# A linear-attention and RWKV feed-forward kernel: other places in the planner's table for about 450 tasks of the first units

## The chip, the cores and the metric

The kernel runs on one core of a Trainium2 chip. A core has five engines that run their own instruction streams: TensorE (PE, matmuls; PEld are its weight loads), VectorE (DVE), ScalarE (ACT), GpSimd (POOL) and SyncE (SP), which here issues all DMA transfers; 16 DMA engines move the data. The metric is the device time of one execution in microseconds (us).

## The reference

For 4 sequences, 8 heads, 768 steps and head size 48, a recurrent attention with a decay per channel is computed, and its output goes through an RWKV channel mix (shift, two mixes, a squared-ReLU feed-forward and a gate).

```python
def _attn_ref(q, k, v, f_logit):
    f = 1.0 / (1.0 + np.exp(-f_logit))
    for t in range(S):
        state = f[:, :, t, :, None] * state + np.einsum('bhd,bhe->bhde', k[:, :, t], v[:, :, t])
        y[:, :, t] = np.einsum('bhd,bhde->bhe', q[:, :, t], state)
def _moe_ref(x, mu_k, mu_r, w_k, w_v, w_r):      # x: (4, 768, 384), w_k: (384, 1024), w_v: (1024, 384)
    xk = mu_k * x + (1.0 - mu_k) * x_prev        # x_prev: x one step earlier
    xr = mu_r * x + (1.0 - mu_r) * x_prev
    k = np.maximum(xk @ w_k, 0.0)
    v = k * k @ w_v
    r = 1.0 / (1.0 + np.exp(-(xr @ w_r)))
    return r * v
```

The weights arrive as 64-bit floats.

## The kernel before, in words

The 4 x 768 steps are cut into 24 chunks of 128 steps (i = 0 to 23; all 8 heads at once), and three chunks make a unit of 384 steps (u = 0 to 7). Each chunk is computed in the parallel form; the state goes from chunk to chunk. Every small job is a task with a name, one engine or a choice of two, an estimated duration, and a place. The names that the text uses:

- Loads on SyncE's queue: `wr0` to `wr3`, `wk0` to `wk7`, `wv0` to `wv5` (pieces of the weights), `f0.0` to `f0.2`, `f1`, `f2` (decay logits of a unit), `qk{i}`, `v{i}` (a chunk's operands), `cst` (the unit matrix `ident` and the mask), `sp{u}.{j}` (small copies that spread two heads' output from `stage` into `x`).
- Weights, on VectorE: three integer operations a piece, as `wkS2`, `wkT2`, `wkX2` (lines 623, 632, 635), turn a 64-bit piece into 32-bit floats; then ScalarE rounds it (`wkH2`, line 638) and GpSimd takes the rest (`wkL2`, line 642). The last product needs `wvL5`.
- Attention of chunk i: `b{i}` scan of the decay and `bl{i}` its last column, `ln{i}`, `rb{i}` its inverse, `q{i}`, `n{i}`, `kr{i}`, `k{i}` scaled operands, `TR{i}` transposes of k (TensorE, line 310), `kt{i}` their copy (lines 314, 315), `SP{i}` scores and state sums (lines 325 and 345, 64 matmul records), `m{i}` the mask (line 337), `zb{i}`, `za{i}`, `T{i}` the state, `YA{i}` and `YB{i}` the output (line 362), with the small copy `w{i}` (lines 381, 382) between them, and `y{i}`, the copy of the output to `x` and `stage` (lines 394, 396).
- Mix of unit u: `d`, `xm` (lines 474, 477, 482), `xh` (rounded, lines 490, 491), `xl` (the rest, line 497). Products on TensorE (line 505): `F{u}.0` to `.7` with wk (9 records each), `R{u}.0` to `.2` with wr (9), `W{u}.00` to `.21` with wv (12); between them `r`, `h`, `kk`, `l` (squares), `lg`, `sg` (gate) and `o`, `out`. W0.01 is unit 0's first row block, second half.
- Fills (line 700): matmuls of `ident` by itself with no use, put into TensorE's waits.

Nothing is decided at run time. A planner (class `Plan`) runs while the program is built: `schedule` takes from all tasks whose predecessors are planned the one with the least key, and the order so found is fixed on every engine.

```python
self.tasks[name] = (name, place + PLACE.get(name, 0.0), ways, tuple(after), tuple(takes), tuple(uses))
...
k = (round((start + 0.2 * stay) / 0.15), place, n)
```

The start in the key is the planner's own estimate, in steps of 0.15; the place (about the number of the unit, less for what should come early) decides between tasks of one step. Where a task can run on two engines, `pick` takes the one that would end first, with `DEAR` added to VectorE's and ScalarE's ends. The buffers of each tag (four PSUM buffers `pm`, four operand buffers `qk`, two `words` buffers) are given out in the planned order, and a task waits until the buffer that it takes is free. The fills go in ahead of a TensorE task whose planned start leaves a gap; they start by `t = max(free["P"], read, FILL[0])`, which does not look at when `ident` lands.

Of the kernel before, what the change touches and what calls it, by code (L numbers as in the profile page):

```python
# [51 lines left out]
AWAY = 1  # L52
SPLIT = True
HALVED = 1
PLACE = {"f1": -0.627, "f2": 0.21, "sf2": -1.016, "qk0": 0.854, "qk1": -0.278, "qk2": 0.127, "qk3": 0.31, "v0": -0.151, "v1": -0.224, "cst": 0.482, "mu": 0.138, "f3": -1.807}
CHECK = (2.0, 0.2)
DEAR = {"V": 2.498, "A": 2.512}


class Plan:  # L60
# [8 lines left out]
    def add(self, name, place, *ways, after=(), takes=(), uses=()):  # L69
        assert name not in self.tasks, name  # L70
        self.tasks[name] = (name, place + PLACE.get(name, 0.0), ways, tuple(after), tuple(takes), tuple(uses))
        for b in (*takes, *uses):
# [11 lines left out]
    def schedule(self, trace=None):  # L84
# [23 lines left out]
        while ready:  # L108
            best = None
            for n, names in ready.items():  # L110
# [6 lines left out]
                at = {w[0]: max([at] + [0.0 if way_of[m] == w[0] else end[m] for m in names]) for w in ways}  # L117
                pick = min(((max(at[w[0]], free[w[0]]) + w[1] + DEAR.get(w[0], 0.0), w) for w in ways), key=lambda x: x[0])[1]
                start = max(at[pick[0]], free[pick[0]])
# [825 lines left out]
```

## Time and profile before

| | |
|---|---|
| Time, median of 3 runs | 357.0 us (356.54 to 357.54) |
| Span of the profiled execution | 354.9 us |
| The rest of the median, around the span | 2.1 us |
| TensorE busy | 323.3 us (91% of the span) |
| VectorE busy | 254.9 us (72%) |
| ScalarE busy | 204.8 us (58%) |
| GpSimd busy | 194.2 us (55%) |
| Mean granted clock of TensorE | 0.988 |

The span is the time from the first to the last instruction of one execution that was profiled; its own time was not taken apart from it, and the median of the three runs stands beside it. Shares are means over the whole span, and the stretches differ: in the first 75 us the weights are turned and the first chunks computed, later the products follow each other.

### The profile page before, as it was taken

How to read it: one execution, taken by the hardware profiler on the slowest of the kernel's cores; microseconds unless marked ns; L12 is line 12 of the kernel's file. 1: busy time of each engine (PE TensorE's matmuls, PEld its weight loads, DVE VectorE, ACT ScalarE, POOL GpSimd, SP SyncE). 2: the span in 40 equal slices, each digit the busy share in tenths (PEclk: the TensorE clock that was granted, in tenths of full speed). 3: DMA queues.
4: the chain of work that ended last, by engine and by line, in shares of the span. 5: the costliest groups of instructions: out<-in, count | busy, mean ns of one | idle time of the engine just before them, and what ended most of it. 6: DMA issues, size and time to landing. Idle time of an engine off the chain costs nothing.

```text
span 354.9 us, 10867 instructions
## 1 busy us (share of the span) xinstructions
PE 323.3 (91%) x4482; PEld 307.0 (87%) x4482; DVE 254.9 (72%) x511; ACT 204.8 (58%) x415; POOL 194.2 (55%) x235
## 2 busy tenths in 40 slices
PE   0395788999999999999999999999999999999993
PEld 0384677888899999999999999999999999999993
DVE  7978799989899878958897598748872943723210
ACT  4686458757476927863575547573876146605520
POOL 2554469986689347724595268625680634634400
PEclk9999699999999999999999999999999999999998
DMA  8999172336521284368524562031401100010001
GB/s 279 403 375 369 54 230 61 118 96 207 204 98 59 55 298 130 105 228 254 170 81 129 187 218 85 2 121 61 152 0 40 48 27 11 8 46 22 3 24 52
DMA packets 20650, 45.32 MB, mean 128 GB/s; under 512 B 2928, under 2 KB 13040, under 8 KB 20592
## 3 DMA queue, kind: packets, MB, share of 16 engines
q1 hardware_dynamic: 20592, 44.55, 37.8%
q8 instruction: 37, 0.61, 0.7%
q14 instruction: 21, 0.17, 0.2%
HBM read 38.64 MB, written 4.72 MB: 122 GB/s over the span
## 4 chain that ended last, share of the span: by engine, by line
PE 70%; DVE 13%; DMA 5%; ACT 4%; issue 3%; POOL 2%; SPq 1%; DVEq 0%; POOLq 0%; ACTq 0%
PE pm L505 56%; PE py L362 6%; PE pss L325 3%; PE pm L310 2%; DMA f<-in_zt 2%; PE pss L345 2%; DVE pm L632 2%; DVE pm L623 2%; DMA qk<-in_qkt 1%; DVE xm L482 1%; DMA words<-in_wv 1%; DVE words L635 1%; DVE xm L477 1%; DVE ss L337 1%; DVE xh L491 1%
## 5 line engine op out<-in xcount | busy, mean ns | idle before, releaser
L505 PE MATMUL pm<-xh,wk 128*128 128x384 f32 x384 | 105.5, 344 | 1.7 <-POOL wk L642 1.1
L505 PE MATMUL pm<-wv,k2h 128*128 128x384 f32 x384 | 98.8, 338 | 0.0
L543 POOL TENSOR_TENSOR k2l<-kk,k2h 128x384 fp32r<-128x384 f32 x64 | 68.1, 1066 | 37.4 <-DVE kk L535 16.3
L497 POOL TENSOR_TENSOR xl<-xm,xh 128x384 fp32r<-128x384 f32 x48 | 52.7, 1101 | 59.7 <-DVE xh L491 49.5
L505 PEld LDWEIGHTS pm<-xh,wk 128*128 128x128 f32 x384 | 69.8, 188 | 5.0 <-POOL wk L642 2.1
L505 PEld LDWEIGHTS pm<-wv,k2h 128*128 128x128 f32 x384 | 68.7, 188 | 0.2
L505 PE MATMUL pm<-xl,wk 128*128 128x384 f32 x192 | 64.6, 336 | 0.0
L505 PE MATMUL pm<-wv,k2l 128*128 128x384 f32 x192 | 64.5, 336 | 0.0
L528 ACT ACTIVATE r<-pm 128x384 f32<-128x384 f32 x54 | 26.5, 491 | 29.8 <-PE pm L505 29.1
L505 PE MATMUL pm<-wr,xh 128*128 128x384 f32 x144 | 38.0, 345 | 0.9 <-DVE words L635 0.9
L595 DVE TENSOR_TENSOR o<-pm,lg 128x384 f32<-128x384 f32 x24 | 13.3, 554 | 34.1 <-PE pm L505 34.1
L505 PEld LDWEIGHTS pm<-wv,k2l 128*128 128x128 f32 x192 | 36.1, 188 | 0.0
L505 PEld LDWEIGHTS pm<-xl,wk 128*128 128x128 f32 x192 | 36.1, 188 | 0.0
L535 DVE SCALAR_TENSOR_TENSOR kk<-pm,r 128x384 f32<-128x384 f32 x39 | 21.6, 555 | 19.6 <-ACT r L528 18.9
L533 ACT ACTIVATE k2h<-r 128x384 fp32r<-128x384 f32 x64 | 33.6, 524 | 3.7 <-DVE r L529 1.4
L240 DVE TENSOR_TENSOR_SCAN pm<-f,low 128x512 f32<-128x512 f32 x24 | 32.1, 1339 | 0.0
L362 PEld LDWEIGHTS py<-qk,z 64*64 64x64 f32 x704 | 16.8, 139 | 15.3 <-issue 7.5
L362 PE MATMUL py<-qk,z 64*64 64x64 f32 x704 | 23.1, 234 | 7.2 <-ACT stage L394 2.8
L394 ACT ACTIVATE x<-py 64x128 f32<-64x128 f32 (+1 forms) x60 | 18.6, 310 | 15.5 <-PE py L362 14.6
L505 PEld LDWEIGHTS pm<-wr,xh 128*128 128x128 f32 x144 | 25.2, 188 | 1.8 <-DVE words L635 1.0
L482 DVE SCALAR_TENSOR_TENSOR xm<-pm,mu_sb,x 128x384 f32<-128x384 f32 x42 | 25.7, 613 | 0.7
L700 PE MATMUL py<-ident 128*128 128x64 f32 x72 | 11.4, 322 | 14.6 <-DVE pm L240 14.6
(101 smaller groups left out, 569.1 us busy)
## 6 DMA issues: line engine op xcount, KB each, us to landing
qk<-in_qkt SPq DMA_DIRECT2D x24, 512.0 KB, 4.5
words<-in_wv SPq DMA_DIRECT2D x12, 512.0 KB, 4.8
f<-in_zt SPq DMA_DIRECT2D x7, 768.0 KB, 5.9
v<-in_vt SPq DMA_DIRECT2D x24, 192.0 KB, 3.1
out<-o SPq DMA_DIRECT2D x24, 192.0 KB, 2.5
words<-in_wk SPq DMA_DIRECT2D x6, 512.0 KB, 5.1
words_k2h<-in_wk SPq DMA_DIRECT2D x4, 384.0 KB, 8.6
words_k2l<-in_wk SPq DMA_DIRECT2D x4, 384.0 KB, 9.5
```

The source lines that it names most:

```text
L240: pl.add(f"b{i}", ga, ("V", 1.25, 1, lambda: nc.vector.tensor_tensor_scan(b().rearrange(FL), f().rearrange(FL), self.low.rearrange(FL), 1. ...
L362: first[c, h] = nc.tensor.matmul(to, lhs, rhs, start=(c, h) not in first, stop=stop, skip_group_check=True)
L394: e.activation(o, i_, AF.Copy, scale=-1.0)
L482: pl.add(f"xm{u}.{n}{j}", pr, ("V", 0.62, 0, lambda xm=xm, n=n, j=j: nc.vector.scalar_tensor_tensor(xm(), pm("d", u, j)[:, :UT], self.mu_s ...
L497: e.tensor_tensor(lo(), xm(), hi().bitcast(F32), op=ALU.subtract)
L505: nc.tensor.matmul(ps, lhs(a, j), rhs(bb, j), start=ends[0] and i == 0, stop=ends[1] and i == len(pr) - 1)
L528: pl.add(f"r{u}.{f}", kf, ("A", 0.5, 0, lambda r=r, ps=ps: nc.scalar.activation(r(), ps(), AF.Relu)), ("V", 0.56, 0, lambda r=r, ps=ps: nc ...
L533: pl.add(f"h{u}.{f}", kf, ("A", 0.53, 0, lambda r=r, hi=hi: nc.scalar.activation(hi(), r(), AF.Square)), after=[f"r{u}.{f}"], **kw)
L535: pl.add(f"kk{u}.{f}", kf, ("V", 0.56, 0, lambda r=r, ps=ps, kk=kk: nc.vector.scalar_tensor_tensor(kk(), ps(), 0.0, r(), op0=ALU.max, op1= ...
L543: e.tensor_tensor(lo(), kk(), hi().bitcast(F32), op=ALU.subtract)
L595: pl.add(f"o{u}.{t}", kv, ("V", 0.56, 0, lambda t=t, ps=ps, o=o: nc.vector.tensor_tensor(o(), ps(), lg()[:, t], op=ALU.mult)), after=[f"W{ ...
L700: self.nc.tensor.matmul(self.py[:, 0, 256:320], self.ident, self.ident[:, :64], start=False, stop=True, skip_group_check=True)
```

## The change

Two constants of the planner change, and no task, instruction, buffer or wait rule. `PLACE` held an offset for 12 tasks; now it holds one for about 450, in the attention of chunks 0 to 11, the weights, unit 0 and most of unit 1. `DEAR` changes in its second digit.

```diff
-PLACE = {"f1": -0.627, "f2": 0.21, "sf2": -1.016, "qk0": 0.854, "qk1": -0.278, "qk2": 0.127, "qk3": 0.31, "v0": -0.151, "v1": -0.224, "cst": 0.482, "mu": 0.138, "f3": -1.807}
+PLACE = {
+    "cst": 0.45, "ex": 7.598, "c0": 0.906, "cm0": -1.376, "c2": -1.069, "v0": -3.667, "b0": 0.122, "bl0": -1.422, "rb0": 0.016,
...
+    "YB3": 0.435, "y3": -4.0, "qk4": 1.56, "v4": -0.449, "b4": -0.062, "bl4": -1.34, "ln4": -1.489, "rb4": 2.257, "kr4": 3.283,
...
 CHECK = (2.0, 0.2)
-DEAR = {"V": 2.498, "A": 2.512}
+DEAR = {"V": 2.455, "A": 2.357}
```

What it moves is seen in the orders. (Line numbers of the changed program are 53 higher, since the table is longer.)

On SyncE's queue, the loads of the first microseconds before the change, from the first decay logits (`f`) on; the four pieces of `wr` (`lg` and `x` are their places) stand ahead of these rows:

```order
L410 DMA f_61<-in_zt 128x512 x3
L228 DMA qk_65<-in_qkt 128x1024
L230 DMA v_101<-in_vt 128x384
L410 DMA f_62<-in_zt 128x1536
L230 DMA v_102<-in_vt 128x384
L228 DMA qk_66<-in_qkt 128x1024
L706 DMA ident<-in_cst 128x128
L708 DMA mask<-in_cst 64x64 x2
L228 DMA qk_64<-in_qkt 128x1024
L230 DMA v_103<-in_vt 128x384
L410 DMA f_63<-in_zt 128x1536
```

and the same place after it, where two pieces of `wr` and `v0` stand ahead:

```order
L682 DMA lg_119<-in_wr 128x576 x2
L463 DMA f_61<-in_zt 128x512 x2
L281 DMA qk_65<-in_qkt 128x1024
L463 DMA f_61<-in_zt 128x512
L463 DMA f_62<-in_zt 128x1536
L281 DMA qk_64<-in_qkt 128x1024
L281 DMA qk_66<-in_qkt 128x1024
L283 DMA v_102<-in_vt 128x384
L283 DMA v_103<-in_vt 128x384
L463 DMA f_63<-in_zt 128x1536
L759 DMA ident<-in_cst 128x128
L761 DMA mask<-in_cst 64x64 x2
```

`ident` and the mask moved from behind `qk2` to behind `f2`; `qk0` moved ahead of them.

On TensorE, the output of chunk 2 and the scores of chunk 3 before the change; `qk_66` is chunk 2's operand, `qk_67` chunk 3's, and the rows from `z_72` on are YB2:

```order
L325 MATMUL pss<-qk_67 64x64 x16
L345 MATMUL pss<-v_101,ktk_100 48x48 x16
L362 MATMUL py<-qk_66,z_72 64x64
L362 MATMUL py<-qk_66,z_73 64x64 x2
L362 MATMUL py<-qk_66,z_72 64x64 x2
L362 MATMUL py<-qk_66,z_73 64x64 x2
L362 MATMUL py<-qk_66,z_72 64x64
L362 MATMUL py<-ss_97,v_103 48x64 x16
L362 MATMUL py<-qk_67,z_75 64x64
```

and after it:

```order
L415 MATMUL py<-qk_66,z_72 64x64
L415 MATMUL py<-qk_66,z_73 64x64 x2
L415 MATMUL py<-qk_66,z_72 64x64 x2
L415 MATMUL py<-qk_66,z_73 64x64 x2
L415 MATMUL py<-qk_66,z_72 64x64
L415 MATMUL py<-ss_97,v_102 48x64 x16
L378 MATMUL pss<-qk_67 64x64 x16
L398 MATMUL pss<-v_101,ktk_100 48x48 x16
L415 MATMUL py<-qk_67,z_75 64x64
```

YB2 now stands ahead of SP3, and so does the copy y2 that follows it. Up to YA2 TensorE's order is unchanged.

On VectorE, the end of chunk 5's operand and the start of unit 0's mix before the change (`ktk_99` is kt4, `qk_65` k5, `words_120` wvT0; `xm` and `xh` are the mix, `ss` and `z` m4 and zb4):

```order
L315 COPY ktk_99<-pm_92 128x384
L262 SCALAR_TENSOR_TENSOR qk_65<-pm_94,qk_65 128x2x128
L266 SCALAR_TENSOR_TENSOR qk_65<-pm_94,qk_65 128x2x64 x2
L632 SCALAR_TENSOR_TENSOR pm_93<-words_120,pm_93 128x512
L477 SCALAR_TENSOR_TENSOR xm_109<-x_105,one_mu,pm_91 128x384
L491 CAST xh_122<-xm_109 128x384
L337 TENSOR_TENSOR ss_97<-pss,mask 128x512
L296 TENSOR_TENSOR z_73<-pss,z_72 128x4x48
L477 SCALAR_TENSOR_TENSOR xm_110<-x_105,one_mu,pm_91 128x384
L491 CAST xh_122<-xm_110 128x384
L477 SCALAR_TENSOR_TENSOR xm_111<-x_105,one_mu,pm_92 128x384
L491 CAST xh_122<-xm_111 128x384
```

and after it:

```order
L315 SCALAR_TENSOR_TENSOR qk_65<-pm_94,qk_65 128x2x128
L319 SCALAR_TENSOR_TENSOR qk_65<-pm_94,qk_65 128x2x64 x2
L685 SCALAR_TENSOR_TENSOR pm_92<-words_120,pm_92 128x512
L530 SCALAR_TENSOR_TENSOR xm_109<-x_105,one_mu,pm_93 128x384
L530 SCALAR_TENSOR_TENSOR xm_110<-x_105,one_mu,pm_94 128x384
L530 SCALAR_TENSOR_TENSOR xm_111<-x_105,one_mu,pm_91 128x384
L390 TENSOR_TENSOR ss_97<-pss,mask 128x512
L349 TENSOR_TENSOR z_73<-pss,z_72 128x4x48
L355 TENSOR_TENSOR sm<-pss,z_73 128x192
L530 SCALAR_TENSOR_TENSOR xm_112<-x_105,one_mu,pm_94 128x384
L544 CAST xh_122<-xm_112 128x384
```

kt4 and three of the xh copies left VectorE for ScalarE. In the same way y5 and the small copy bl6 go to ScalarE, and kk0.7 comes to VectorE. Between the xm rows and wkX7 VectorE's list of weight pieces is the same but for wv4, which stands where wv2 stood. Further on, YB6, SP7 and YA7 come later among the products of units 0 and 1, and some 30 tasks of all units have another engine. Of the nine fills seven are left: five stood among F0.1 to F0.7, now three.

## Rows read from the trace of the kernel before

**Rows 1.** The page: busy us and instructions by engine; the instruction queue: packets, MB, share.
```profile
PE 323.3 (91%) x4482; PEld 307.0 (87%) x4482; DVE 254.9 (72%) x511; ACT 204.8 (58%) x415; POOL 194.2 (55%) x235
...
q8 instruction: 37, 0.61, 0.7%
```

**Rows 2.** Windows: busy us (instructions) per engine, granted TensorE clock, DMA share, GB/s.
```profile
36.00:39.00 3.00, 3.00 (x125) 3.00 (x125) 2.07 (x5) 0.55 (x1) 2.15 (x3) 0.53 0.07 23
...
75.00:350.00 275.00, 273.53 (x3568) 262.42 (x3566) 189.13 (x380) 155.18 (x313) 147.80 (x173) 1.00 0.31 102
```

**Rows 3.** Timeline of TensorE: start us, us, engine line op out<-in xcount [idle before].
```profile
14.57 3.65 PE L700 MATMUL py<-ident 128*128 128x64 f32 x16 [14.57 <-DVE pm L240]
...
19.08 1.97 PE L310 MATMUL pm<-ident,qk 128*128 128x128 f32 x8 [0.86 <-DVE qk L266]
...
29.74 0.66 PE L310 MATMUL pm<-ident,qk 128*128 128x128 f32 x4
...
30.55 0.46 PE L362 MATMUL py<-qk,z 64*64 64x64 f32 x16 [0.15 <-ACT done L381]
...
33.45 0.29 PE L362 MATMUL py<-qk,z 64*64 64x64 f32 x3 [0.58 <-DVE z L296]
...
35.91 0.59 PE L362 MATMUL py<-qk,z 64*64 64x64 f32 x11 [2.16 <-issue]
...
80.57 0.59 PE L505 MATMUL pm<-wv,k2h 128*128 128x384 f32 x2
...
95.39 0.45 PE L505 MATMUL pm<-xh,wk 128*128 128x384 f32 x1
```

**Rows 4.** Timeline of GpSimd.
```profile
79.37 1.31 POOL L642 TENSOR_TENSOR wv<-words,wv 128x512 fp32r<-128x512 f32 x1 [1.22 <-ACT wv L638]
...
93.40 1.78 POOL L497 TENSOR_TENSOR xl<-xm,xh 128x384 fp32r<-128x384 f32 x1 [0.36 <-DVE xh L491]
```

**Rows 5.** Timeline of VectorE.
```profile
38.16 0.69 DVE L337 TENSOR_TENSOR ss<-pss,mask 128x512 f32<-128x512 f32 x1 [0.22 <-PE pss L345]
...
43.31 0.56 DVE L315 COPY ktk<-pm 128x384 f32<-128x384 f32 x1 [0.48 <-PE pm L310]
...
45.10 0.61 DVE L477 SCALAR_TENSOR_TENSOR xm<-x,one_mu,pm 128x384 f32<-128x384 f32 x1
...
53.14 0.55 DVE L623 TENSOR_SCALAR pm<-words_k2l 128x384 int32<-128x384 int32 x1
...
74.31 1.04 DVE L396 TENSOR_SCALAR x<-py 128x256 f32<-128x256 f32 x3
...
76.40 0.69 DVE L623 TENSOR_SCALAR pm<-words 128x512 int32<-128x512 int32 x1 [0.74 <-DMA words<-in_wv]
...
77.92 0.69 DVE L635 SCALAR_TENSOR_TENSOR words<-words,pm 128x512 int32<-128x512 int32 x1
```

**Rows 6.** Timeline of SyncE's queue, two DMA issues.
```profile
7.29 0.33 SPq L706 DMA_DIRECT2D ident<-in_cst  x1
...
12.31 0.33 SPq L410 DMA_DIRECT2D f<-in_zt  x1
```

**Rows 7.** DMA issues from 7.2 and from 12.3 us: KB each, us to landing.
```profile
ident<-in_cst SPq DMA_DIRECT2D x1, 64.0 KB, 7.1
...
f<-in_zt SPq DMA_DIRECT2D x1, 768.0 KB, 5.9
```

**Rows 8.** The instruction queue in 33.4 to 33.5 and in 37.0 to 37.1 us.
```profile
q8 instruction: 1, 0.02, 68.0%
...
q8 instruction: 1, 0.02, 65.5%
```

**Rows 9.** Timeline of ScalarE: the copy y2 begins.
```profile
39.27 0.97 ACT L394 ACTIVATE x<-py 128x256 f32<-128x256 f32 x3 [1.34 <-PE py L362]
```

**Rows 10.** Tile xh on VectorE: ns min/median/max, first and last start.
```profile
L491 DVE CAST xh<-xm x36: 355/396/999, 45.7 to 312.3; 128x384 fp32r<-128x384 f32 x36
```

**Rows 11.** The chain that ended last: start us, us, what.
```profile
103.61 9.71 PE pm L505 x54
```

More of the change, by code (lines that the diff above doesn't have):

```diff
@@ L54 @@
 HALVED = 1
-PLACE = {"f1": -0.627, "f2": 0.21, "sf2": -1.016, "qk0": 0.854, "qk1": -0.278, "qk2": 0.127, "qk3": 0.31, "v0": -0.151, "v1": -0.224, "cst": 0.482, "mu": 0.138, "f3": -1.807}
+PLACE = {
[52 rows of a table added]
+}
 CHECK = (2.0, 0.2)
-DEAR = {"V": 2.498, "A": 2.512}
+DEAR = {"V": 2.455, "A": 2.357}
 class Plan:
```

50 rows, old and new, of the table PLACE are left out of this document.

## The prediction

> **What bounds the kernel now.** I read the page's busy times and the windows first: the reader is to see two regimes. From 75 to 350 us TensorE is busy for 273.5 of 275 us, at the full granted clock; in the first 75 us, by the difference to the page's totals, it is busy for 323.3 - 273.5 = 49.8, and VectorE for 254.9 - 189.1 = 65.8 [rows 1, 2]. So every microsecond that the kernel can gain or lose lies before about 80 us: TensorE's work is fixed, and the time is set by how soon it becomes unbroken. Next the timeline of TensorE, for the places where it stands still or waits [rows 3]; then the DMA queue and VectorE's timeline, for what it stands still for. The place where the early part hands over is W0.01 (the second half of the first product with wv), which starts at 80.57 [rows 3], just when GpSimd ends wvL5, the last step of the last piece of wv, at 79.37 + 1.31 = 80.7 [rows 4]. So what counts is when VectorE ends wvX5, now 77.92 + 0.69 = 78.6 [rows 5]. All steps below are times of the profiled execution (span 354.9). The median of the runs is 357.0, 2.1 more, which I keep as what lies around the span.
>
> **Step 1, ident comes later.** On SyncE's queue ident is now issued behind v2, v1, f2, qk0 and qk2; ahead of it stand just the loads that stand up to f2 before the change, without ident and the masks themselves. ident was issued at 7.29 and landed 7.1 later, at 14.4; f2 at 12.31 + 5.9 = 18.2 [rows 6, 7]. So ident lands at about 18.2. The first instructions of TensorE are two fills, 16 records that read ident and take 3.65 us; they began at 14.57, as ident landed, and TR0 came at 19.08 [rows 3]. Both orders have the fills ahead of TR0. Now 18.2 + 3.65 = 21.85: TR0 is late by 2.8 us, though its operand (k0) is ready as before. The bounds are 0 (if so small a load overtakes the large ones) and 2.8; I take 2.8, because the landings of the two loads follow the order of issue.
>
> **Step 2, the chain of the first three chunks carries it.** Up to YB1 each step of TensorE waits for ScalarE, GpSimd or VectorE, which waited for TensorE; the order of these steps is the same. YB1 goes from 30.55 [rows 3] to 33.3. The loads are the same in number, so nothing there is shorter.
>
> **Step 3, the stop in YA2.** Before, YA2 starts at 33.45, runs three records and then stands for 2.16 us, for nothing that the profile shows [rows 3]. I read this as a wait for instructions. TensorE's 4482 matmuls and as many weight loads came in about 37 packets of its instruction queue, some 121 matmuls to a packet [rows 1]. By the program's order the stop is at record 347, so the block was to be asked for one block earlier, near record 226, where TR2 (29.74) gives way to YB1 (30.55) [rows 3]. Its packet ran at 33.4, 2.9 to 3.7 us after that, while the loads had the DMA engines full; the next one ran at 37.0, only 1.1 after the restart at 35.91 [rows 3, 8]. From request to restart it was 35.91 - 30.55 = 5.4 to 35.91 - 29.74 = 6.2; with an idle queue 1.8 to 2.6 less, so 3.6 both ways. Now the request comes 2.8 later, at 32.5 to 33.3, when most of the loads are through: restart at 36.1 to 36.9 with an idle queue, up to 38.7 with one as full as before. I take 36.5, the middle of the idle case: 0.6 after the old restart, not 2.8. The stop has taken up most of the delay of step 1.
>
> The Trainium skill (Runtime: NRT & Kernel Launch, "Instruction fetch mechanics") says that an engine gets its instructions in 16 KiB blocks on a DMA queue of its own, and that the cost of a block's edge is mostly hidden. The packets of 0.02 MB agree; the 2.16 us do not agree with "mostly hidden". By the page there would be no such stop, and the sum would be that of the first rival.
>
> **Step 4, YB2 now ahead of SP3.** From the restart to the copy y2 it was 39.27 - 35.91 = 3.36 us [rows 3, 9], with the 64 records of SP3 in between. In 36 to 39 us TensorE ran 125 records in 3.0 us, at a granted clock of 0.53, near the lower level of 1.2 GHz, after it had stood still [rows 2]: 64 of them are 1.5 us. The wait for the small copy w2, which SP3 covered, is now bare: 0.2. y2 at 36.5 + 3.36 - 1.5 + 0.2 = 38.6, 0.7 earlier. The price: SP3 now ends 1.5 later, at about 40.0, and VectorE's m3, which waits for SP3, starts there and not at 38.16 [rows 5]: +1.9.
>
> **Step 5, VectorE up to the weights.** From m3 to the first xm it was 45.10 - 38.16 = 6.94 us, with the copy kt4 (0.56) and a wait of 0.48 ahead of it [rows 5]. kt4 goes to ScalarE: 1.0 less. The first xm is at 40.05 + 5.9 = 46.0, +0.9. From there to wkS2 it was 8.04 us (53.14) [rows 5]; three xh copies go to ScalarE, at 0.36 each at least [rows 10]: 1.0 less. wkS2 starts at 53.0, -0.1. ScalarE has the room: 204.8 - 155.2 = 49.6 of 75 us busy [rows 1, 2]. Bounds for the copies: 0 if the next xm waits anyway, and 3 x 1.0, since one such copy took up to 0.999 us [rows 10].
>
> Why one copy takes nearly three times as long as another, the row does not say. The Trainium skill (SBUF — State Buffer, "SBUF: two separate sides") has VectorE and GpSimd share one port pair that locks for a whole instruction. By that rule the three copies would be worth up to 3.0 and not 1.0, and the sum would be up to 2 us better.
>
> **Step 6, the weights.** From wkS2 to wkX7 VectorE's list has the same pieces, wv4 in place of wv2. From there to wvX5, y5 goes to ScalarE and with it the wait for wv5's load: from 74.31 to 76.40, 2.1 us [rows 5]. wv5's slot now comes free from wv2, not from the piece just before it. kk0.7 (ScalarE before) and n6 now stand ahead of wvX5: 0.56 by the copy kt4, which has kk's 384 columns, and 0.69 by m3, which has n6's 512 [rows 5], 1.2 together. Net -0.9; the small copy bl6 is 0.1 more. wvX5 at 78.6 - 0.1 - 1.0 = 77.5, so wvL5 is 1.1 earlier. TensorE must be as early: R0.2 now takes the PSUM buffer that wvX3 leaves, and wvX3 ends three operations ahead of the end of wvX5, 2.1 us by 0.69 each [rows 5], at 75.4; then R0.2 (9 records) and W0.00 (12) at 9.71 / 54 = 0.18 a record [rows 11] and TR6 make 4.3, and W0.01 comes at 79.7. It was 80.57; I take 0.9 earlier.
>
> **Step 7, after W0.01.** The product tasks are the same. TensorE's idle time from 75 to 350 is 275 - 273.5 = 1.5 us in all, its end included [rows 2]; I take 0.3 of it back, since YA7 and SP7, which stand next to F1.0, come later now and wait less. Sum: -0.9 - 0.3 = -1.2 us, span 353.7, time **355.8**. Its own range is 354.8 to 356.8, the restart of step 3 up or down by 1.
>
> **Rivals.** *No stop in YA2.* Then YA2 runs at 33.45 + 2.8 = 36.2, at the full clock: 125 records in 1.5 and not 3.0 us, and VectorE is 1.5 to 1.8 earlier. For it: with most loads through, the packet can be there in time. Against it: even an idle queue needed 3.6 from request to restart, and YA2 comes 2.9 to 3.7 after the request. 355.8 - 1.5 = 354.3.
>
> *The late ident decides (slower).* The stop follows the request as long as before: restart at 38.7 and not 36.5, so m3, the first xm and wkS2 are 2.2 later than in my sum, and nothing behind gives it back: -1.2 + 2.2 = +1.0; with an eighth of the 2.0 relief of steps 5 and 6 lost besides, +1.3: 358.3. My sum is spent from a start of m3 at 41.2 on. For it: v3 and qk4 wait for YB0 and so come 2.8 later too, into the time of the request. Against it: they are two loads, not the whole list. Its upper end is the 2.8 of step 1 with no relief at all: 359.8.
>
> *A new wait eats the gain.* F1.0 starts at 95.39, and its last operand was ready at 93.40 + 1.78 = 95.18 [rows 3, 4]: only 0.2 to spare. If TensorE comes 1.2 earlier and the mix of unit 1 does not, it waits, and the time is 357.0 - 0.2 = 356.8. Against it: y5 no longer waits on VectorE, and the spread loads follow it. Some 30 tasks further on have other engines and places, each a chance of such a wait.
>
> **How the numbers follow.** Chances: my sum 0.41, no stop 0.18, new wait 0.17, late ident 0.24. About 0.3% (1.1 us) is what a measurement of this kernel can tell from no change. Of my sum's range somewhat over half lies below 355.9: 0.24, and with the 0.18 of the first rival and 0.04 of the third 0.46 is faster. Same: 0.17 of my sum and 0.13 of the third rival, 0.30. Slower 0.24. The range runs from 353.5, under the first rival, to 358.5, over the second: about 0.1 is left out at each end.
>
> **What would show it.** Right: the first fill at 18.2 and TR0 at 21.9; a stop in YA2 that ends at 36 to 37; y2 before 39; m3 at 40; wkS2 within 0.5 of 53.1; W0.01 near 79.7; TensorE unbroken from there. Wrong: the first fill before 16 (step 1 falls, and the time is better by up to 2); a restart after 38; wkS2 after 54; waits of TensorE of more than 1 us in all after 80.

## The result

The changed kernel takes 353.5 us (median of 6, 352.7 to 355.6), the kernel before 357.1 beside it: a ratio of 0.9907, with a 95% interval of 0.9878 to 0.9936. It is faster, by some 3.3 us (2.3 to 4.4), where I had forecast 355.8 and a range from 353.5: the sign is right, the size was off by more than two. That the time lies on the lower end of the range, and not outside it, is luck: I had drawn that end for the first rival, and it was not that rival that brought it there. The profiled execution has a span of 351.8, 3.1 less than before. (`PLACE` now holds 405 offsets, not about 450.)

The page of the changed kernel, busy us by engine [rows 1]:

```profile
PE 318.8 (91%) x4466; PEld 303.7 (86%) x4466; DVE 247.6 (70%) x489; ACT 213.8 (61%) x437; POOL 195.3 (55%) x235
```

Its timeline of TensorE, at the places of [rows 3]: the first fills, TR0, YB1, YA2 with its restart, W0.01 with a wait inside it, F1.0.

```profile
19.09 3.65 PE L753 MATMUL py<-ident 128*128 128x64 f32 x16 [19.09 <-DVE pm L323]
22.53 1.91 PE L363 MATMUL pm<-ident,qk 128*128 128x128 f32 x8
...
33.94 0.46 PE L415 MATMUL py<-qk,z 64*64 64x64 f32 x16
...
36.34 0.30 PE L415 MATMUL py<-qk,z 64*64 64x64 f32 x3
37.13 0.45 PE L415 MATMUL py<-qk,z 64*64 64x64 f32 x13 [0.50 <-issue]
...
78.92 0.60 PE L558 MATMUL pm<-wv,k2h 128*128 128x384 f32 x2
...
80.58 0.44 PE L558 MATMUL pm<-wv,k2h 128*128 128x384 f32 x1 [0.19 <-POOL wv L695]
...
93.09 0.33 PE L558 MATMUL pm<-xh,wk 128*128 128x384 f32 x1
```

Its timeline of VectorE [rows 5]: m3, three xm in a row, the two xh copies that are left, wkS2, kk0.7, wvS5, wvX5, the scan b7.

```profile
40.02 0.68 DVE L390 TENSOR_TENSOR ss<-pss,mask 128x512 f32<-128x512 f32 x1
...
46.13 1.66 DVE L530 SCALAR_TENSOR_TENSOR xm<-x,one_mu,pm 128x384 f32<-128x384 f32 x3
...
49.59 0.41 DVE L544 CAST xh<-xm 128x384 fp32r<-128x384 f32 x1
...
51.69 0.37 DVE L544 CAST xh<-xm 128x384 fp32r<-128x384 f32 x1
51.98 0.55 DVE L676 TENSOR_SCALAR pm<-words_k2l 128x384 int32<-128x384 int32 x1
...
72.40 0.56 DVE L588 SCALAR_TENSOR_TENSOR kk<-pm,r 128x384 f32<-128x384 f32 x1 [0.77 <-POOL k2l L596]
...
75.41 0.69 DVE L676 TENSOR_SCALAR pm<-words 128x512 int32<-128x512 int32 x1 [0.66 <-DMA words<-in_wv]
...
76.87 0.69 DVE L688 SCALAR_TENSOR_TENSOR words<-words,pm 128x512 int32<-128x512 int32 x1
...
78.20 1.22 DVE L293 TENSOR_TENSOR_SCAN pm<-f,low 128x512 f32<-128x512 f32 x1
```

GpSimd's timeline, with za5 and two xl beside those copies, a weight piece beside wkS2, the fourth piece of wv, and wvL5; below it wv5's load on SyncE's queue:

```profile
49.27 0.52 POOL L343 TENSOR_TENSOR z<-sm,g 128x192 f32<-128x192 f32 x1
49.74 2.10 POOL L550 TENSOR_TENSOR xl<-xm,xh 128x384 fp32r<-128x384 f32 x2
51.81 1.43 POOL L695 TENSOR_TENSOR wv<-words,wv 128x512 fp32r<-128x512 f32 x1
...
69.08 2.33 POOL L695 TENSOR_TENSOR wv<-words,wv 128x512 fp32r<-128x512 f32 x1
...
78.32 2.20 POOL L695 TENSOR_TENSOR wv<-words,wv 128x512 fp32r<-128x512 f32 x1 [1.34 <-ACT wv L691]
```

```profile
71.44 0.33 SPq L682 DMA_DIRECT2D words<-in_wv  x1
```

Windows of the changed kernel [rows 2]:

```profile
36.00:39.00 3.00, 2.09 (x92) 1.64 (x93) 2.31 (x7) 2.27 (x7) 2.22 (x4) 1.00 0.78 238
75.00:350.00 275.00, 270.64 (x3560) 260.91 (x3559) 184.21 (x362) 161.79 (x327) 147.17 (x171) 1.00 0.31 101
```

Read downward, these rows say where the time went. The start is 3.45 later (TR0), the restart in YA2 only 1.2 later, since the stop is 0.50 and not 2.16, and the granted clock of 36 to 39 is 1.00 and not 0.53. The first xm is 1.0 later, wkS2 already 1.2 earlier: from the one to the other it is 5.85 us where it was 8.04. wvX5 is 1.05 earlier. SP6, which follows W0.01, starts at 81.64 where it was 82.83, and TensorE's last record at 345.92 where it was 348.92: 1.2 of these 3.0 us arise ahead of SP6. The other 1.8 arise behind it, where I had put 0.3.

### The profile page after: what moved, and what is told of

The parts are those of the page before. It is cut to its first block, busy times and chain, and to the rows that moved or that the text cites. A ratio compares the mean times of both kernels' runs of the same rounds, so it can differ in the third digit from the quotient of the medians.

```text
span 351.8 us, 10835 instructions
## 1 busy us (share of the span) xinstructions
PE 318.8 (91%) x4466; PEld 303.7 (86%) x4466; DVE 247.6 (70%) x489; ACT 213.8 (61%) x437; POOL 195.3 (55%) x235
## 4 chain that ended last, share of the span: by engine, by line
PE 75%; DVE 10%; DMA 3%; ACT 3%; POOL 3%; issue 2%; SPq 1%; DVEq 0%; POOLq 0%
PE pm L558 60%; PE py L415 6%; PE pss L378 3%; PE pm L363 3%; DMA f<-in_zt 2%; DVE pm L685 2%; PE pss L398 2%; DVE pm L676 2%; PE py L753 2%; POOL wv L695 1%; DMA words<-in_wv 1%; DVE words L688 1%; DVE xm L535 1%; DVE words_k2l L688 1%; POOL k2l L596 1%
## 5 line engine op out<-in xcount | busy, mean ns | idle before, releaser
L550 POOL TENSOR_TENSOR xl<-xm,xh 128x384 fp32r<-128x384 f32 x48 | 50.3, 1057 | 50.2 <-ACT xh L543 24.6
L581 ACT ACTIVATE r<-pm 128x384 f32<-128x384 f32 x56 | 27.5, 490 | 24.9 <-PE pm L558 23.5
L586 ACT ACTIVATE k2h<-r 128x384 fp32r<-128x384 f32 x64 | 33.5, 526 | 5.2 <-DVE r L582 3.3
L588 DVE SCALAR_TENSOR_TENSOR kk<-pm,r 128x384 f32<-128x384 f32 x34 | 18.9, 555 | 22.6 <-ACT r L581 21.6
L293 DVE TENSOR_TENSOR_SCAN pm<-f,low 128x512 f32<-128x512 f32 x24 | 33.4, 1392 | 0.2 <-ACT ktk L367 0.2
L447 ACT ACTIVATE x<-py 64x128 f32<-64x128 f32 (+1 forms) x69 | 21.4, 309 | 18.3 <-PE py L415 16.6
L753 PE MATMUL py<-ident 128*128 128x64 f32 x56 | 9.6, 335 | 19.1 <-DVE pm L323 19.1
```

Of the source, the lines that this page charges most:

```text
L293: pl.add(f"b{i}", ga, ("V", 1.25, 1, lambda: nc.vector.tensor_tensor_scan(b().rearrange(FL), f().rearrange(FL), self.low.rearrange(FL), 1. ...
L447: e.activation(o, i_, AF.Copy, scale=-1.0)
L550: e.tensor_tensor(lo(), xm(), hi().bitcast(F32), op=ALU.subtract)
L581: pl.add(f"r{u}.{f}", kf, ("A", 0.5, 0, lambda r=r, ps=ps: nc.scalar.activation(r(), ps(), AF.Relu)), ("V", 0.56, 0, lambda r=r, ps=ps: nc ...
L586: pl.add(f"h{u}.{f}", kf, ("A", 0.53, 0, lambda r=r, hi=hi: nc.scalar.activation(hi(), r(), AF.Square)), after=[f"r{u}.{f}"], **kw)
L588: pl.add(f"kk{u}.{f}", kf, ("V", 0.56, 0, lambda r=r, ps=ps, kk=kk: nc.vector.scalar_tensor_tensor(kk(), ps(), 0.0, r(), op0=ALU.max, op1= ...
```

## The experiments

There are twelve, and they are named by their numbers further on. In all but the fifth, one or a few tasks are moved in the finished order (in the eighth and ninth an instruction is changed as well). `moved` takes the planned list, puts a task just ahead of another on its engine (`ahead`), or gives it to another engine (`ways`), and sorts the list again so that every dependency holds; nothing else is planned anew. The first edit is shown whole, of the others the arguments alone.

**1. Ident early (changed kernel).**

```diff
-    k.emit(plan.schedule())
+    k.emit(moved(plan, plan.schedule(), ahead=[('cst', 'qk0')]))
```

> The changed kernel with one task moved: ident and the masks are issued ahead of qk0 on SyncE's queue, about where they stood before the change. Theory A (the chain takes up the delay at its fetch stop and at later waits): fills and TR0 come about 3.4 us earlier than in the changed kernel (TR0 near 19.1), YA2 starts near 33.5 and stands again for 1.5 to 2.5 us at its third record, m3 starts 0 to 1.2 earlier than 40.02, and the time falls by 0 to 1 us: 352.5 to 353.5. Rival B (the late ident costs its whole delay, so the change would have gained 3 more without it): m3 near 36.7 and the time near 350.3. Rival C (ident ahead of the big loads holds those up): TR0 early, but v1, qk0 or qk2 land later and the time is 353.5 or more.

Measured: 353.4 us, ratio 0.9915 (0.9886 to 0.9943), so no gain over the changed kernel that can be told. Timeline of TensorE in YA2:

```profile
34.78 0.34 PE L415 MATMUL py<-qk,z 64*64 64x64 f32 x3
36.29 0.45 PE L415 MATMUL py<-qk,z 64*64 64x64 f32 x13 [1.17 <-issue]
```

TR0 is 2.7 earlier, the restart and m3 0.84, SP6 0.9: the stop takes up two thirds of what the early ident gives, as A has it. Against the second profile of the changed kernel (experiment 5) record 347, where the restart is, and SP6 are only 0.2 earlier.

**2. Ident late (kernel before).**

```diff
+    k.emit(moved(plan, plan.schedule(), ahead=[('cst', 'qk3')]))
```

> The kernel before with one task moved: ident and the masks are issued behind f2, as in the change; all else as before. Theory A: TR0 3 to 3.5 later than 19.08, but the restart in YA2 only about 1.2 later than 35.91 (near 37.1), since the stop shrinks to about 0.5; SP3 still stands ahead of YB2, so m3 is near 39.4 and W0.01 up to 1.2 later; the time is 0.3 to 1.2 us over before. Rival B (late ident decides): W0.01 2.5 to 3.4 later than 80.57 and the time 2.5 to 3.4 over before. Rival C (nothing, the xm part has slack): W0.01 within 0.2 of 80.57 and the same time.

Measured: 357.4 us, ratio 1.0027 (1.0008 to 1.0045), 1.0 us over before (0.3 to 1.6). In its profile TR0 is 3.1 later and the restart 0.6 (36.51, after stops of 0.60 in YA1 and 0.84 in YA2), and SP6 is at 82.82, level with before. B, the late ident that costs its delay, is refuted by both; between A (by the times) and C (by the profile) the run does not decide.

**3. Bundles apart (changed kernel).** The edit for chunk 8; the same for 11, 14, 17 and 20:

```diff
+    ahead=[('SP9', 'W1.00'), ('YB8', 'W1.01'), ...]
```

> The changed kernel with TensorE's order altered at five places (chunks 8, 11, 14, 17, 20): the bundle YA, SP, YB, which stood between two product tasks, is taken apart, so that SP stands one product task later and YB two. The work is the same, TensorE crosses from product matmuls to attention matmuls and back ten times more. Theory A (each crossing and return costs TensorE some 0.43 us besides the work: 268 ns instead of 173 from the last product record, 80 more at the fourth attention record, 148 back, about 110 more at the first product record): the time rises by 4.3 us to about 357.8, with no wait of TensorE on another engine over 0.5 in all. Rival B (crossings are free, the microseconds after W0.01 came from waits): the time stays within 0.5 of the changed kernel, 353.0 to 354.0, or TensorE shows new waits of its own that make up the rise.

Measured: 361.2 us, ratio 1.0118 (1.0093 to 1.0144), 7.5 over the changed kernel. Timeline of TensorE around one of the new visits, then where it newly waits:

```profile
114.91 0.34 PE L558 MATMUL pm<-wr,xl 128*128 128x384 f32 x1
115.17 0.69 PE L378 MATMUL pss<-qk 64*64 64x64 f32 x32
115.69 0.54 PE L398 MATMUL pss<-v,ktk 64*48 64x48 f32 x32
116.16 0.62 PE L558 MATMUL pm<-wv,k2h 128*128 128x384 f32 x2
116.61 0.33 PE L558 MATMUL pm<-wv,k2l 128*128 128x384 f32 x1
...
134.79 0.44 PE L558 MATMUL pm<-xh,wk 128*128 128x384 f32 x1 [1.37 <-issue]
...
168.88 0.66 PE L363 MATMUL pm<-ident,qk 128*128 128x128 f32 x4 [0.94 <-DVE o L648]
```

Starts are to be read here, and a visit is a stretch of attention matmuls between two products. The step into the visit takes 0.26 (a product to the next takes 0.17), the first two products behind it 0.45 (0.35 elsewhere). From R1.1 to W1.10 it is 111.28 to 121.47, 10.19 us; in the changed kernel 111.32 to 120.80, 9.48. Two more visits cost 0.71, **0.36 each**, and ten 3.6; the same stretch in the next four units gives 0.71 or 0.72 each time. So a visit has a price, a little under A's 0.43. The other 3.9 are for the most part waits that came with the moves (a stop of 1.5 in F2.0, and TR13, TR16 and TR22 for VectorE), which A had excluded.

**4. Bundles joined (kernel before).**

```diff
+    ahead=[('YB6', 'W0.21'), ('TR8', 'F1.2'), ('YA7', 'SP8'), ('YB7', 'F1.3'), ('w7', 'h1.2'), ('y7', 'h1.3')]
```

> The kernel before with TensorE's order altered between W0.20 and F1.3 alone: YB6 goes behind TR7, TR8 ahead of F1.2, and YA7, SP8 and YB7 stand as one bundle ahead of F1.3; so there are six visits to attention matmuls where there were eight, as in the change. On ScalarE w7 and y7 move back to match. Theory A (crossings): from W0.01 to R1.0 the stretch is 0.86 shorter by two crossings and 0.2 more by the wait ahead of YA7, about 1.0 in all; the time is 356.1 where before is 357.1, and the part up to W0.01 is as before. Rival B (the stretch was shorter because something else, such as VectorE's order or a load, was early): the stretch from W0.01 (80.57) to R1.0 (111.60) stays within 0.3 of 31.0. A wait of F1.3 to F1.6 for the moved tasks would hide theory A; it would show as TensorE's wait.

Measured: 358.0 us, ratio 1.0046 (1.0026 to 1.0066). Timeline of TensorE:

```profile
98.47 0.66 PE L310 MATMUL pm<-ident,qk 128*128 128x128 f32 x4 [0.59 <-DVE qk L266]
...
103.03 0.46 PE L362 MATMUL py<-qk,z 64*64 64x64 f32 x16 [0.99 <-ACT done L381]
```

A miss: the stretch from SP6 to R1.0 is 29.9 us where it was 28.8. TR8 now waits for VectorE and YB7 for ScalarE, whose orders were made for the old places; by their starts the two lose 1.9, and less two visits (0.7) that is the 1.1. It shows that the joining alone does not pay; in the changed kernel, whose other engines have other orders too, neither wait is there.

**5. The changed kernel again.** No edit.

> The changed kernel itself, once more, beside the other kernels of this batch. Theory A (the stop of 0.46 us in F2.0 is a stop for instructions that depends on when the block's packet gets through, so it comes in some executions and not in others): the profile has W7.21 within 0.6 of 344.01, and wherever TensorE stops for nothing that the profile shows, it goes on 2.2 to 2.4 us after a packet of its instruction queue. Rival B (the stops belong to fixed places of the order): the same stop of 0.4 to 0.5 at the fourth record of F2.0, near 133. The time is 353.5, up or down by 1.

Measured: 353.7 us, ratio 0.9878 (0.9845 to 0.9912); span 351.6. The stop in F2.0 comes again at the same record, its 1745th matmul, 0.39 by its start (0.46 before). In experiments 1 and 6 it does not come; so the place is fixed, as B has it, and the size is not, as A has it. The first microseconds are not the same either:

```profile
31.75 0.47 PE L415 MATMUL py<-qk,z 64*64 64x64 f32 x2 [1.37 <-issue]
```

This is in YA1, at record 222, one block ahead of the stop in YA2. TensorE is at YA1 2.8 earlier here (29.93 for 32.74), stops there for 1.37 us, until 2.70 after the block's packet (29.05; A had 2.2 to 2.4), and then runs through YA2 without a stop: record 347 starts at 36.52 (37.13). In the other experiments with the changed order and ident late (3 and 6 to 10) it is like this too: 0.91 to 1.75 in YA1, no stop over 0.15 in YA2.

**6. SP3 ahead of YB2 (changed kernel).**

```diff
+    ahead=[('SP3', 'YB2')]
```

> The changed kernel with SP3 ahead of YB2 again, as before the change. Theory A (what counts is y2, whose spread loads the first mix waits for; m3 has weight work of VectorE ahead of it and does not wait for SP3): y2 starts about 0.9 later than 38.91, m3 stays within 0.2 of 40.02, the first xm comes 0.5 to 0.8 later than 46.13, and the time rises by 0.3 to 0.8 us. Rival B (the price of my step 4 was real, m3 is set by SP3): m3 1.0 earlier, the first xm not later than 46.13, and the time 0 to 1 us lower.

Measured: 354.2 us, ratio 0.9908 (0.9876 to 0.9940), 0.5 over the run beside it, which the intervals do not tell from nothing. VectorE:

```profile
40.03 0.68 DVE L390 TENSOR_TENSOR ss<-pss,mask 128x512 f32<-128x512 f32 x1
...
46.45 1.67 DVE L530 SCALAR_TENSOR_TENSOR xm<-x,one_mu,pm 128x384 f32<-128x384 f32 x3 [0.23 <-ACT pm L527]
```

m3 does not move, though SP3 starts 1.2 earlier: it stands behind weight pieces, with no wait, 2.32 after w2 (37.71) as in both profiles of the changed kernel (37.70 and 37.09). y2 starts at 39.28 (38.91 and 38.29), and the first xm now waits and comes 0.3 later than in the first profile, 0.9 later than in the second. A by its mechanism; the size is not settled.

**7. Three copies back on VectorE (changed kernel).**

```diff
+    ahead=[('xh0.00', 'xm0.01'), ('xh0.01', 'xm0.10'), ('xh0.10', 'm4')], ways={'xh0.00': 'V', 'xh0.01': 'V', 'xh0.10': 'V'}
```

> The changed kernel with three copies xh0.00, xh0.01 and xh0.10 back on VectorE, each behind its xm as before the change; ScalarE no longer does them. Theory A (a copy of VectorE that starts while GpSimd is in an instruction ends about 0.2 after that instruction ends, in the kernel before 0.36, 0.36, 0.74, 0.47 and 1.00): the copies take 0.36 only where GpSimd is idle, their five together 2.2 to 3.4 us where the two of the changed kernel take 0.78, wkS2 is 1.5 to 2.5 later than 51.98, and the time rises by 0.8 to 2.0 us. Rival B (my sum's fixed 0.36 each): the five together take 1.8, wkS2 is 1.0 later, and the time rises by 0.5 to 1.0.

Measured: 356.1 us, ratio 0.9951 (0.9929 to 0.9972), 2.4 over the changed kernel beside it. VectorE's five copies and wkS2, then GpSimd's two xl that run beside the second and the third:

```profile
47.22 0.36 DVE L544 CAST xh<-xm 128x384 fp32r<-128x384 f32 x1
...
48.14 0.73 DVE L544 CAST xh<-xm 128x384 fp32r<-128x384 f32 x1
...
49.43 0.73 DVE L544 CAST xh<-xm 128x384 fp32r<-128x384 f32 x1
...
51.98 0.36 DVE L544 CAST xh<-xm 128x384 fp32r<-128x384 f32 x1
...
54.02 0.36 DVE L544 CAST xh<-xm 128x384 fp32r<-128x384 f32 x1
54.30 0.55 DVE L676 TENSOR_SCALAR pm<-words_k2l 128x384 int32<-128x384 int32 x1
```

```profile
47.66 1.00 POOL L550 TENSOR_TENSOR xl<-xm,xh 128x384 fp32r<-128x384 f32 x1 [1.12 <-DVE xh L544]
48.95 0.99 POOL L550 TENSOR_TENSOR xl<-xm,xh 128x384 fp32r<-128x384 f32 x1 [0.30 <-DVE xh L544]
```

48.14 + 0.73 = 48.87 is 0.21 after the xl ends (48.66); 49.43 + 0.73 = 50.16 is 0.22 after the next (49.94). The five make 2.54; wkS2 is 2.3 later than 51.98, and from the first xm to it 7.73 us pass, not 5.85. A holds, though the time rises by 2.4 and not by 2.0 at most; B's 1.0 does not.

**8. The copies with two operands.**

```diff
-                       ("V", 0.4, 1, lambda xm=xm, hi=hi: nc.vector.tensor_copy(hi(), xm())),
+                       ("V", 0.4, 1, lambda xm=xm, hi=hi: nc.vector.tensor_tensor(hi(), xm(), xm(), op=ALU.max)),
```

> As the kernel with the three copies back on VectorE, but each of VectorE's xh copies is written as the maximum of xm with itself, an operation with two operands. Theory A (it is the one-operand copy that waits for GpSimd, as xm, m3 and the weight words with two operands never took longer beside it): all copies take the same 0.55 to 0.62 us, whatever GpSimd does, none over 0.65. Rival B (any instruction of VectorE that writes xh while GpSimd works on the same tiles waits): some take 0.7 to 1.0, as in the copies. The time is within 0.5 us of the kernel with the copies back, by either theory, since five times 0.58 make 2.9.

Measured: 356.8 us, ratio 0.9976 (0.9953 to 0.9998). Two of VectorE's five:

```profile
47.31 0.56 DVE L544 TENSOR_TENSOR xh<-xm 128x384 fp32r<-128x384 f32 x1
...
48.43 0.93 DVE L544 TENSOR_TENSOR xh<-xm 128x384 fp32r<-128x384 f32 x1
```

A fell: beside an xl the two-operand form takes 0.93 too, twice. So what sets the copies apart is not that they have one operand. The five make 3.54 and not 2.9, and the time is 0.7 over that of experiment 7, where both theories had 0.5 at most.

**9. The copies from PSUM.** The instruction of xm writes xh as well (and xm0.11 goes ahead of xm0.12, so that its xh follows it):

```diff
+                        for to in (xm, hi) if both else (xm,):
+                            nc.vector.scalar_tensor_tensor(
+                                to(), x()[:, j, :UT], self.one_mu[:, n, j : j + 1], pm("d", u, n, j)[:, :UT],
+                                op0=ALU.mult, op1=ALU.add)
...
```

> As the kernel with the three copies back on VectorE, but each of VectorE's five xh tiles of unit 0 is not copied from xm: the instruction that computes xm (one operand in SBUF, one in PSUM) is run a second time with xh as its output. Theory A (an instruction of VectorE waits for GpSimd only when all that it reads is in SBUF; the copies of 0.73 and the two-operand forms of 0.93 did, xm with its PSUM operand never took over 0.62): all ten instructions take 0.55 to 0.65 us, also where an xl of GpSimd runs beside them; wkS2 is 0.2 to 0.8 later than in the kernel with the copies back (54.30), since five times 0.58 is more than the 2.54 that the copies took. Rival B (what writes xh waits for GpSimd, whatever it reads): the second ones take 0.7 to 1.0 beside an xl. The Trainium skill (SBUF — State Buffer, "SBUF: two separate sides") says that a VectorE instruction takes the pair of ports that it shares with GpSimd when it runs in a two-port mode or has two inputs in SBUF; theory A would agree with it.

Measured: 355.9 us, ratio 0.9953 (0.9933 to 0.9972). VectorE, then GpSimd beside it:

```profile
47.76 0.61 DVE L534 SCALAR_TENSOR_TENSOR xh<-x,one_mu,pm 128x384 fp32r<-128x384 f32 x1
```

```profile
47.40 2.04 POOL L556 TENSOR_TENSOR xl<-xm,xh 128x384 fp32r<-128x384 f32 x2 [0.83 <-DVE xh L534]
```

All ten take 0.60 or 0.61, also beside an xl. What writes xh does not wait if one of its inputs is in PSUM; the copies and the two-operand forms, which read SBUF alone, did. But not every instruction that reads SBUF alone waits: wkS2, whose one input is in SBUF and whose output is in PSUM, keeps its 0.55 beside GpSimd's 1.43 in the changed kernel (51.98 and 51.81). Only the forecast that wkS2 would be later failed: it is at 53.80, since such instructions start 0.53 apart.

**10. y5 back on VectorE (changed kernel).**

```diff
+    ahead=[('y5', 'wvS5')], ways={'y5': 'V'}
```

> The changed kernel with y5, the copy of chunk 5's output, back on VectorE just ahead of wvS5. Theory A (step 6: y5 costs VectorE its 1.2 us, of which 0.66 lie in the wait for wv5's load): wvS5 starts 0.4 to 0.7 later than 75.41, W0.01 ends 0.3 to 0.7 later than 81.71, and the time rises by 0.3 to 0.7 us. Rival B (wvL5 is late for another reason, GpSimd's 2.20 beside VectorE's scan b7, so that the shift only moves the scan): wvL5 ends within 0.2 of 80.52 and the time stays the same within 0.3.

Measured: 354.5 us, ratio 0.9917 (0.9888 to 0.9946), which is not told from the changed kernel's. wvS5 starts at 75.37 right behind y5, with no wait for its load, and SP6 at 81.60. In the changed kernel's second profile, whose F0.0 starts as early as here (50.45, 50.58), wvS5 is at 74.73 and SP6 at 80.96, which is for A; in its first profile they are at 75.41 and 81.64, which is for B. The two profiles differ from each other by as much as A forecasts, so the run does not decide.

**11. Ident early, one copy more away (changed kernel).**

```diff
+    ahead=[('cst', 'qk0'), ('xh0.11', 'y4')], ways={'xh0.11': 'A'}
```

> The changed kernel with two tasks moved: ident and the masks are issued ahead of qk0, and the copy xh0.11, which VectorE still does, goes to ScalarE, behind xh0.12 and ahead of y4. Theory A (both are on VectorE's chain up to wvX5): SP6 starts 0.9 earlier than 81.64 by the first and 0.35 earlier by the second, near 80.4; the span is 350.2 to 350.8 and the time 352.2 to 353.0. Rival B (VectorE waits for wv5's load anyway, or y4 and r0.0, which come 0.5 later on ScalarE, cost as much): SP6 at 80.7 or later, and the time 353.4 or more, as with ident alone.

Measured: 354.5 us, ratio 0.9912 (0.9885 to 0.9939): no better. Its windows:

```profile
36.00:40.00 4.00, 2.80 (x93) 2.61 (x96) 2.25 (x5) 0.55 (x4) 1.69 (x4) 0.54 0.31 120
40.00:44.00 4.00, 2.56 (x88) 2.24 (x86) 2.93 (x7) 1.37 (x5) 2.70 (x4) 0.50 0.28 75
```

From the first xm to wkS2 it takes 5.46, 0.4 less as meant. But YA2, early again, stands for 2.36 us, the clock is at its lower level until 44, m3 waits 0.93 for SP3, and SP6 is at 82.69. B's numbers came, but for neither of its reasons; the early ident gives no sure gain.

**12. The copies alone (kernel before).**

```diff
+    ahead=[('xh0.00', 'd0.02'), ('xh0.01', 'd0.11'), ('xh0.10', 'y4')], ways={'xh0.00': 'A', 'xh0.01': 'A', 'xh0.10': 'A'}
```

> The kernel before with one part of the change alone: the three copies xh0.00, xh0.01 and xh0.10 go from VectorE to ScalarE (behind d0.01, d0.02 and d0.12 there); ident, TensorE's order and all else as before. Theory A (the copies that leave and the waits for GpSimd of the two that stay were the largest part of the gain up to W0.01): VectorE's two remaining copies take 0.36 to 0.75 each, wkS2 is 1.3 to 2.2 earlier than 53.14, SP6 starts 0.8 to 2.0 earlier than 82.83, and the time falls by 0.8 to 2.0 us against before. Rival B (my sum's 1.0 for the copies, with the wait for wv5's load behind it): wkS2 1.0 earlier, SP6 at most 0.4 earlier, and the time within 0.5 of before.

Measured: 356.2 us, ratio 0.9958 (0.9932 to 0.9983), 1.5 under before. SP6 is 1.2 earlier. Of VectorE's two copies one takes longer than ever, from 47.91 to 0.21 after an xl that started with it and ended at 48.91:

```profile
47.91 1.21 DVE L491 CAST xh<-xm 128x384 fp32r<-128x384 f32 x1
```

A by the time and SP6, though its copies were to take 0.75 at most; wkS2 (51.94, 1.2 earlier) lies between A and B, as two xm now wait 0.67 for ScalarE, whose order was not made for the copies. SP6 comes at 81.66, where the whole change has it at 81.64; from there to the last record it takes 266.3 us, as in the kernel before (266.1).

## Why the prediction had the sign and not the size

**Step 1** held: the fills begin at 19.09 and TR0 at 22.53, 3.45 later and not 2.8; ident took 8.4 us to land. **Step 2** held (YB1 33.94; I had 33.3).

**Step 3** held by its end, and by its mechanism in part. Record 347 starts at 37.13 in one profile of the changed kernel and at 36.52 in the other; I had 36.5. But the stop in YA2 that I had there is 0.50 in the first and missing in the second, which stops one block earlier, in YA1 (experiment 5). What holds in all profiles is that a stop follows the packet of TensorE's instruction queue: packet at 33.5 and restart at 35.91 before [rows 3, 8], 34.8 and 37.13 after, 33.8 and 36.29 with ident early, 34.3 and 36.87 in experiment 11. That is 2.3 to 2.6 us each time, and 2.5 to 2.7 at the stops in YA1. The Trainium skill (Runtime: NRT & Kernel Launch, "Instruction fetch mechanics") has the next 16 KiB block, 256 instructions, fetched while the current one runs. The trace agrees with the size: the stops at records 222, 1745 and 3526 lie 1, 11 and 25 times 127 from the one at 347, to within 4 records; 127 matmuls with as many weight loads make 254. It calls the cost mostly hidden. By the starts of records 127 apart, that holds for the blocks with many products, which last some 6 us and more; at blocks of almost only attention matmuls, which TensorE runs through in 3 to 4.4, it did not always hold.

**Step 4**: y2 came at 38.91 (38.6) and m3 at 40.02 (40.05), but not for my reason. SP3 is not what m3 waits for. Four weight operations now stand between w2 and m3 where there were two, so the +1.9 was no price of the exchange (experiment 6).

**Step 5** is the first of three mis-sized terms. I gave the three copies 1.0; from the first xm to wkS2 the gain was 2.2 (8.04 to 5.85), and experiment 7 gives back 1.9 of it, 2.4 us of the time. The three that left had taken 0.36, 0.36 and 0.47, so 1.2: my price was nearly right. What I had missed is that the two that stayed got faster as well, 0.74 and 1.00 before, 0.41 and 0.37 after: the other 1.0. I did not look at what GpSimd did beside the long ones. The longest before, on VectorE, and GpSimd's xl beside it:

```profile
51.10 1.00 DVE L491 CAST xh<-xm 128x384 fp32r<-128x384 f32 x1
```

```profile
50.87 1.01 POOL L497 TENSOR_TENSOR xl<-xm,xh 128x384 fp32r<-128x384 f32 x1
```

It ends at 52.10, 0.22 after the xl (51.88), and so do the others that took over 0.36. The Trainium skill's rule (SBUF — State Buffer, "SBUF: two separate sides"), which I had named and set aside, is the one that the traces bear out: it makes an instruction of VectorE with two inputs in SBUF wait (experiments 8 and 9), and one in a two-port mode. That the copies run in such a mode no run here shows. The part is worth 1.5 us by itself in the kernel before (0.6 to 2.4; experiment 12).

**Step 6** is the second, and its end came out by luck: wvX5 ends at 77.56, where I had 77.5, but wkS2 was 1.2 earlier, where I had 0.1, and from there to the end of wvX5 it takes 25.6 us where it was 25.5; I had 1.0 less. Two errors cancelled. What left VectorE's list (y5) and what came to it does not show, because wv5's load binds wvS5 in both kernels (waits of 0.74 and 0.66). That load is issued as GpSimd ends the fourth piece of wv: after the change at 71.44 (69.08 + 2.33 = 71.41), and before it, as 70.26 + 2.32 = 72.58, at

```profile
72.60 0.33 SPq L629 DMA_DIRECT2D words<-in_wv  x1
```

The load is 1.16 earlier, just what wkS2 had gained. kk0.7, now on VectorE, waits 0.77 for GpSimd besides, which that wait for the load hides. From wkS2 to SP6 it is 29.7 us in both kernels: ahead of SP6 nothing but the way to wkS2 paid. wvL5 takes 2.20 and not 1.31, as in all ten profiles of the changed order: the scan b7 starts 0.12 ahead of it. Before, it was wvL5 that started first (79.37, a scan of VectorE at 80.07), and the scan that took 1.70 and not 1.22. W0.01 came at 78.92 with a wait of 0.19 in it; SP6 1.2 earlier, where I had 0.9.

**Step 7** is the third: 0.3 forecast, 1.8 found. I had counted only TensorE's idle time and took its busy time as fixed; but what the page calls busy holds the price of visits. From SP6 to the last record it takes 266.1 us before and 264.3 after. I took, for each kind of step from one record to the next, its median over the two traces, and summed each order: some 0.6 less for the new one. In units 0 and 1, from W0.01 to F1.4, there are six visits where there were eight, and in units 4 and 6 one less each; in units 2, 3 and 5 YB now stands apart and adds one each. That is one visit less in all, 0.36; the other 0.3 come from the two transposes of lot, which stand behind YB20 and no longer between SP21 and YB20. The steps that took over 40 ns more than their median add up to some 2.3 before and 1.3 after, and 0.1 is spread over all steps: among those that went are the wait of YA7 for VectorE (0.24), a stop in YB19 (0.35, from a block's packet at 250.1 to 252.37), and some 0.4 each at F2.4 and F3.4; among the new ones are the stop in F2.0 and 0.4 at F4.4. That a visit costs 0.36 is shown (experiment 3). What F2.4 waits for is named at its weight load (kernel before):

```profile
142.75 0.19 PEld L505 LDWEIGHTS pm<-xh,wk 128*128 128x128 f32 x1 [0.46 <-DVE qk L266]
```

It is VectorE's end of a scaled k, the last that reads a PSUM buffer of that chunk; at F4.4 after the change it is the same, and at F3.4 it is a kk on VectorE. That moving these would give the 0.4 back was not tried.

**The rivals.** *No stop* in YA2 came in the second profile, but not its gain, since the stop was then in YA1. *The late ident decides* is refuted in its size by experiments 1 and 2, and 11 agrees. *A new wait at F1.0* did not come; F1.0 starts behind W0.21 with no wait.

How sure the parts are: two profiles of the changed kernel differ by 0.7 at SP6, and by 0.2 in the span. The stretches differ less. From the first xm to wkS2 it is 5.85 to 5.87 us in all six profiles with the changed order and the copies away (the changed kernel's first and experiments 1, 3, 5, 6 and 10), and 8.0 to 8.6 in three with the order before (its own and experiments 2 and 4). From SP6 to the last record it is 263.8 to 264.6 in the nine with the changed order but for experiment 3, and 265.7 to 266.3 in the three with the order before but for experiment 4; of that, SP6 to R1.0 is 27.8 and 28.8. So the 1.8 belongs to the order behind SP6, good to some 0.5; about 1.0 of it, up to R1.0, fits two visits less (0.7) and the wait of YA7 (0.24), and the rest is argued from the sums alone.

## What to carry to other kernels

Before costing an instruction that moves from VectorE, look at what GpSimd runs beside it, and beside those that stay: for a copy from SBUF to SBUF, or an instruction with two inputs in SBUF, the price was not its least duration but the rest of GpSimd's instruction. Check a forecast by its terms and not only by its end: here two wrong ones met at the right time. On a TensorE that looks full, count how often it changes between two kinds of matmul, since the change is in its busy time. A delay ahead of a stop for instructions was here mostly free, and one that came away gained as little.

## What the hardware did that I had not expected

- A block's instructions were usable 2.2 to 2.7 us after its packet, in every stop of these runs, and the stop at one record was between 0 and 1.5 us (F2.0) from run to run, as the packet went at 130.8 in one run and 132.6 in another.
- VectorE and GpSimd hold each other up in both directions: a copy of 0.36 took up to 1.21, and GpSimd's wvL5 2.20 and not 1.31 beside a scan that reads f and low, both in SBUF, and had started first; where wvL5 started first, the scan took 1.70 and not 1.22. VectorE's instructions with a PSUM input kept their 0.60, and wkS2, with one input in SBUF and its output in PSUM, its 0.55.
- A visit of TensorE from 128x384 products to 64-row attention matmuls and back costs 0.36 us beside the work, at the full granted clock.
- After the stop of 2.36 us in experiment 11 the granted clock lay at 0.54 and 0.50 for 8 us, near the lower of its two levels (1.2 GHz); after the 0.50 us of the changed kernel it was 1.00.
